# Unread products on row groups and column groups behind the end of a gated attention and feed-forward kernel

## The chip, the cores and the metric

The kernel runs on one core of a Trainium2 chip, in one launch. The metric is the device time of one execution in microseconds. Before the change it is 1037.36 us, the median of 2 runs (1037.11 and 1037.6).

## The reference

One input `x` of 2048 tokens with 448 features goes into two blocks, whose results are mixed token by token by a gate:

```
g = sigmoid((x * gate_w).sum(-1))
qkv = x @ wqkv                          # 448 -> 3 x 16 heads x 28
p = softmax(q @ k.T * 28 ** -0.5)       # 2048 x 2048 for each of 16 heads
a = (p @ v) @ wo                        # back to 448
b = (gelu(x @ w_gate) * (x @ w_up)) @ w_down   # 448 -> 1792 -> 448
out = g * a + (1 - g) * b               # 2048 x 448, float32
```

Everything is float32. The gelu is the tanh approximation.

## The kernel before

The tokens are cut into 4 blocks of 512 (`TB`) or 16 tiles of 128 (`P`). Most products are made in the type `float32r` from operands that were split into a high and a low part, so that one product of the reference is a sum of eleven (`PAIRS`, line 44) products of 128 rows by 128 columns by 512. `X` (line 67) holds the split input with the features on the 128 partitions: seven tiles of 2048 tokens, in a pool that stays to the end. Every product is issued through the helper `mm` (line 53), which pins it: TensorE does the products in the order in which the program writes them. All products therefore have line 54 in the profile, and are told apart by their tiles.

The work comes in three stages.

1. Lines 88 to 264: seven warming products on a tile of zeros (`warm`, line 108), whose result nothing reads; then queries and keys (`pqk`), stored to memory, and values (`pv`), kept in `VA`. A bound on the scores is worked out (`pb`, `pr`, lines 240 and 243), and a branch at line 286 is taken only where it is exceeded.
2. Lines 321 to 453: the attention, head by head. `scores` (line 345) makes a tile `sc` of 128 keys by 1024 queries, ScalarE takes its exponential into `pt`. After each eight key tiles `values` (line 355) multiplies them by the values. These products are in plain float32 and only 32 columns wide: four of them, `j` = 0 to 3, write to four strips of 32 partitions of one accumulator `po` (shown as `ps`), so each stands on its own **column group** of the array. Between the scores the generator `up` (line 394) hands out products of the feed-forward block (`ps<-X,half`), whose results go to memory.
3. Lines 457 to 575: the rest of the feed-forward block and the output. `hidden` makes or reads the gate and up halves of the hidden layer (`pg`), `down` (line 499) multiplies by `w_down` into `pd`, `project` (line 545) multiplies the attention's result by `wo`. The last call, `down(*pend)` at line 575, makes four tiles of `pd`; VectorE mixes each into `y` (line 517) and SyncE's queue stores it (line 518). This is the end of the program.

The accumulators of the last stage are three tiles in the pool `psg` and five in `psd`, which together fill the eight banks of PSUM; its SBUF pools are given back, and with them their addresses, when the block of line 457 is left.

Of the kernel before, what the change touches and what calls it, by code (L numbers as in the profile page):

```python
# [7 lines left out]
F32 = mybir.dt.float32  # L8
# [5 lines left out]
PSUM = bass.MemoryType.PSUM  # L14
# [3 lines left out]
P = 128  # L18
TB = 512
# [555 lines left out]
        down(*pend)  # L575


# [33 lines left out]
```

## Time and profile before

| | |
|---|---|
| median of 2 runs | 1037.36 us |
| the profiled execution's own time | 1038.66 us |
| its span, first to last instruction | 1036.8 us |
| TensorE products busy | 1030.6 us (99%), 5671 products |
| TensorE weight loads busy | 737.6 us (71%) |
| ScalarE / VectorE / GpSimd busy | 603.3 / 325.7 / 195.9 us |
| granted TensorE clock | 1.0 |

PE is TensorE with its products, PEld TensorE with the loads of the operand that is held in the array (each product has one load), DVE VectorE, ACT ScalarE, POOL GpSimd, SP SyncE; SPq is SyncE's queue of transfers. A group of instructions is shown by its line, engine, operation, output and inputs, by the piece of the array (128*128 is all of it, 128*32 is 128 rows by 32 columns), the shape and the count, then the busy time in us and the mean length of one in ns, then the idle time of the engine ahead of it. Records of one group overlap, so the busy time is less than the count times the mean. In the lines of the timeline the first number is the start and the second the length from the start of the first to the end of the last, both in us; x24 means that 24 instructions were merged, and the bracket at the end has the idle time ahead of them.

### The profile page before, as it was taken

What the parts mean: (1) busy time and instruction counts of PE and PEld (TensorE: products, weight loads), DVE (VectorE), ACT (ScalarE), POOL (GpSimd) and SP (SyncE); (2) the same over time, 40 slices, a digit from 0 to 9 for tenths busy, and PEclk for the clock granted to TensorE, in tenths of its full rate; (3) what the DMA queues carried; (4) which work ended last, traced back from release to release, by engine and by line L of the source; (5) the groups of instructions that cost most, each with busy time, mean ns of one, the idle gap of its engine ahead of it and who ended that gap; (6) DMA issues with size and microseconds to landing.
All of it is one profiled execution on the core that took longest, in us unless ns stands there. A gap on an engine that the chain in (4) does not pass through costs nothing.

```text
span 1036.8 us, 14751 instructions
## 1 busy us (share of the span) xinstructions
PE 1030.6 (99%) x5671; PEld 737.6 (71%) x5671; DVE 325.7 (31%) x519; ACT 603.3 (58%) x742; POOL 195.9 (19%) x294
## 2 busy tenths in 40 slices
PE   9999999999999999999999999999999999999998
PEld 7889865666566556655665566556666888888997
DVE  5452011111111111111111111111113687777756
ACT  4332575777577757775777677667763344333322
POOL 6322003021130221211312302202111200001221
PEclk9999999999999999999999999999999999999999
DMA  6865324324234233344242342423124645443553
GB/s 222 315 262 145 78 87 113 103 71 124 75 93 118 83 103 83 88 124 112 71 113 87 96 113 71 115 76 107 53 79 149 175 140 161 140 120 82 160 170 118
DMA packets 59964, 124.25 MB, mean 120 GB/s; under 512 B 11472, under 2 KB 18384, under 8 KB 56272
## 3 DMA queue, kind: packets, MB, share of 16 engines
q1 hardware_dynamic: 50672, 109.99, 35.9%
q0 software_dynamic: 8384, 12.47, 4.5%
q8 instruction: 47, 0.77, 0.3%
q10 hardware_dynamic: 832, 0.79, 0.3%
q14 instruction: 29, 0.24, 0.1%
HBM read 78.64 MB, written 44.56 MB: 119 GB/s over the span
## 4 chain that ended last, share of the span: by engine, by line
PE 88%; DVE 0%; issue 0%
PE ps L54 42%; PE sc L54 23%; PE pd L54 17%; PE pg L54 7%; DVE y L517 0%
## 5 line engine op out<-in xcount | busy, mean ns | idle before, releaser
L352 ACT ACTIVATE pt<-sc 128x1024 f32<-128x1024 f32 x512 | 475.0, 1074 | 188.7 <-PE sc L54 188.4
L54 PE MATMUL sc<-Q,K 128*128 128x512 f32 x1024 | 319.7, 393 | 0.0
L54 PE MATMUL ps<-X,half 128*128 128x512 f32 x924 | 289.7, 391 | 0.1
L54 PEld LDWEIGHTS sc<-Q,K 128*128 128x128 f32 x1024 | 188.8, 188 | 65.2 <-issue 26.0
L54 PE MATMUL ps<-pt,V 128*32 128x512 f32 x2048 | 226.4, 594 | 0.0
L54 PEld LDWEIGHTS ps<-X,half 128*128 128x128 f32 x924 | 173.3, 188 | 38.8 <-issue 1.4
L54 PEld LDWEIGHTS ps<-pt,V 128*32 128x32 f32 x2048 | 63.4, 110 | 145.6 <-issue 144.5
L54 PE MATMUL pd<-w,hl 128*128 128x448 f32 x672 | 140.7, 366 | 0.0
L410 DVE COPY u<-ps 128x512 f32<-128x512 f32 x84 | 57.9, 689 | 256.6 <-PE ps L54 256.5
L54 PEld LDWEIGHTS pd<-w,hl 128*128 128x128 f32 x672 | 126.0, 188 | 11.5
L373 POOL DMA_DIRECT2D dend<-o x64 | 31.8, 505 | 417.7 <-DVE o L364 414.8
L496 ACT ACTIVATE hl<-g 128x512 fp32r<-128x512 f32 x56 | 35.4, 632 | 89.8 <-DVE g L495 80.1
L54 PE MATMUL pg<-X,half 128*128 128x512 f32 x308 | 74.3, 391 | 0.0
L54 PE MATMUL pqk<-X,WQK 128*128 128x512 f32 x308 | 72.8, 399 | 0.9 <-ACT X L152 0.8
L54 PEld LDWEIGHTS pqk<-X,WQK 128*128 128x128 f32 x308 | 59.3, 193 | 14.7 <-ACT X L152 1.5
L54 PEld LDWEIGHTS pg<-X,half 128*128 128x128 f32 x308 | 57.9, 188 | 11.6
L514 DVE SCALAR_TENSOR_TENSOR acc<-pd,gate,acc 128x448 f32<-128x448 f32 x80 | 53.6, 680 | 21.6 <-PE pd L54 21.6
L367 DVE COPY o<-ps 128x512 f32<-128x512 f32 x16 | 11.1, 691 | 148.4 <-PE ps L54 89.2
L364 DVE TENSOR_TENSOR o<-ps,o 128x512 f32<-128x512 f32 x16 | 11.1, 691 | 147.8 <-PE ps L54 147.8
L170 ACT ACTIVATE hl<-pqk 128x512 fp32r<-128x512 f32 x28 | 16.7, 598 | 42.5 <-PE pqk L54 40.5
L497 DVE TENSOR_TENSOR hl<-g,hl 128x512 fp32r<-128x512 f32 x56 | 38.4, 686 | 9.6 <-ACT hl L496 8.5
L495 DVE TENSOR_TENSOR g<-g,u 128x512 f32<-128x512 f32 x56 | 38.0, 686 | 10.5 <-ACT g L494 9.8
(73 smaller groups left out, 528.9 us busy)
## 6 DMA issues: line engine op xcount, KB each, us to landing
ud<-u SPq DMA_DIRECT2D x84, 256.0 KB
qkd<-hl SPq DMA_DIRECT2D x28, 512.0 KB
K<-qkd SPq DMA_DIRECT2D x64, 224.0 KB
Q<-qkd SPq DMA_DIRECT2D x64, 224.0 KB
u<-ud SPq DMA_DIRECT2D x56, 256.0 KB
gs<-ud SPq DMA_DIRECT2D x28, 256.0 KB
rb<-rdend POOLq DMA_DIRECT2D x64, 64.0 KB, 2.9
raw<-in_xT SPq DMA_DIRECT2D x14, 256.0 KB
```

Source lines behind the costliest of these rows:

```text
L54: return pin(nc.tensor.matmul(o, lhsT, rhs, start=start, stop=stop))
L170: pin(nc.scalar.activation(hl[:, 0], p, AF.Copy))
L352: nc.scalar.activation(pt, sc, AF.Exp, scale=SCALE)
L364: nc.vector.tensor_tensor(o, po, o, OP.add)
L367: nc.vector.tensor_copy(o, po)
L373: nc.gpsimd.dma_start(out=dend[h:h + 1, j * 512:(j + 1) * 512], in_=o[j * 32 + DH:j * 32 + DH + 1])
L410: nc.vector.tensor_copy(u, p)
L495: pin(nc.vector.tensor_tensor(g, g, u, OP.mult))
L496: nc.scalar.activation(hl[:, 0], g, AF.Copy)
L497: nc.vector.tensor_tensor(hl[:, 1], g, hl[:, 0].bitcast(F32), OP.subtract)
L514: nc.vector.scalar_tensor_tensor(acc[:, t], p, g1, acc[:, t], OP.mult, OP.add)
```

## The change

Behind the last `down` a further block is added. It takes a new SBUF pool with two tiles of constants, `W` and `R`, and a new PSUM pool with eight accumulators `T` of 128 by 512. Nothing reads `T`. Two helpers issue products:

- `quad` makes one product on each of the **row groups** that it is given: group `r` is partitions 32 r to 32 r + 31. Both operands are slices of `X` on these 32 partitions (128 columns held, 512 streamed, in `float32r`), and the result goes to `T[r]`.
- `run` makes products like those of `values`: plain float32, 128 rows, 32 columns, four of them on the four column groups of `T[4]`, with 256 or 512 columns streamed.

The block calls 126 times `quad` on four groups; then four times a `run` of 8 rounds with 256 columns and 24 `quad`; then twice a `run` of 4 rounds with 512 columns and 12 `quad` with the groups in the order 0, 2, 1, 3; then 24 `quad` on two groups and 24 on three.

```diff
@@ -575,6 +575,43 @@
         down(*pend)
 
 
+    with ExitStack() as ph:
+        bp = ph.enter_context(tc.tile_pool(name="bp", bufs=1))
+        pb4 = ph.enter_context(tc.tile_pool(name="pb4", bufs=1, space=PSUM))
+        T = [pb4.tile([P, TB], F32, name=f"t{i}") for i in range(8)]
+        W = bp.tile([P, 8, 32], F32, name="W")
+        R = bp.tile([P, 8, TB], F32, name="R")
+        nc.vector.memset(W, 0.5)
+        for i in range(4):
+            nc.vector.memset(R[:, 2 * i:2 * i + 2], 0.25)
+
+        def quad(k, n, groups=(0, 1, 2, 3)):
+            for r in groups:
+                a = slice(32 * r, 32 * r + 32)
+                mm(T[r], X[a, (k + r) % 7, (k % 16) * P:(k % 16 + 1) * P],
+                   X[a, (k + 3) % 7, r * TB:(r + 1) * TB], k == 0, k == n - 1)
+
+        def run(kts, n):
+            for k in range(kts):
+                for j in range(4):
+                    mm(T[4][j * 32:(j + 1) * 32, 0:n], W[:, k % 8], R[:, (k + 2 * j) % 8, 0:n], k == 0, k == kts - 1)
+
+        for k in range(126):
+            quad(k, 126)
+        for _ in range(4):
+            run(8, 256)
+            for k in range(24):
+                quad(k, 24)
+        for _ in range(2):
+            run(4, 512)
+            for k in range(12):
+                quad(k, 12, (0, 2, 1, 3))
+        for k in range(24):
+            quad(k, 24, (0, 1))
+        for k in range(24):
+            quad(k, 24, (0, 1, 2))
+
+
```

## The prediction

> **What bounds the kernel now.** I read first the page's span and busy times, then the slices, then the chain of work that ended last, then the groups.
>
> ```profile
> span 1036.8 us, 14751 instructions
> PE 1030.6 (99%) x5671; PEld 737.6 (71%) x5671; DVE 325.7 (31%) x519; ACT 603.3 (58%) x742; POOL 195.9 (19%) x294
> PE   9999999999999999999999999999999999999998
> PEclk9999999999999999999999999999999999999999
> PE 88%; DVE 0%; issue 0%
> PE ps L54 42%; PE sc L54 23%; PE pd L54 17%; PE pg L54 7%; DVE y L517 0%
> ```
>
> TensorE has work in flight for 1030.6 of 1036.8 us, at a full granted clock in every slice, and 88% of the chain lies on it. Work that is added to its queue therefore finds no hole to go into: whatever TensorE needs for it is added to the time, unless it goes behind the last useful product, where a few microseconds of other work are still running. That is where this change puts it. So the question is what stands at the end, and how long TensorE takes for the added products. The timeline of the last stretch (start, length, engine, line, output and inputs, count):
>
> ```profile
> 1027.93 4.85 PEld L54 LDWEIGHTS pd<-w,hl 128*128 128x128 f32 x24
> 1028.13 5.02 PE L54 MATMUL pd<-w,hl 128*128 128x448 f32 x24
> ...
> 1030.26 3.98 SPq L518 DMA_DIRECT2D out<-y  x4
> ...
> 1033.19 0.68 DVE L517 SCALAR_TENSOR_TENSOR y<-pd,gate,acc 128x448 f32<-128x448 f32 x1 [0.53 <-PE pd L54]
> ```
>
> The last product ends at 1028.13 + 5.02 = 1033.15 us, the last VectorE step at 1033.87, and the last store is issued by 1034.24; the rest up to 1036.8 is that store's way to memory. So 1036.8 - 1033.15 = 3.65 us of the span lie behind TensorE's end, and added products run beside them.
>
> **What is added.** Counted from the diff, `quad` is called 126 + 4 x 24 + 2 x 12 = 246 times with four row groups, 24 times with two and 24 times with three: 294 rounds, 984 + 48 + 72 = 1104 products of 32 rows by 128 columns by 512 (the change's few words say about 1650; I go by the diff). `run` adds 4 x 8 rounds of four products with 256 columns and 2 x 4 rounds with 512: 160 products in plain float32, on column groups as `values` has them. Five memsets on VectorE have 30 us or more of products ahead of the first run to hide in; without that cover they would cost a few us once. No transfer is added.
>
> **The price of a product.** No row of before has a product on 32 rows, so it must come from its neighbours: a full product of the same type and 512 columns, and the values, whose four products stand on four column groups.
>
> ```profile
> 779.08 3.56 PE L54 MATMUL ps<-X,half 128*128 128x512 f32 x15
> ...
> 778.86 3.36 PEld L54 LDWEIGHTS ps<-X,half 128*128 128x128 f32 x15
> L54 PE MATMUL ps<-X,half 128*128 128x512 f32 x924 | 289.7, 391 | 0.1
> L54 PEld LDWEIGHTS ps<-X,half 128*128 128x128 f32 x924 | 173.3, 188 | 38.8 <-issue 1.4 <-DVE o L364 0.7 <-DVE o L367 0.4
> L54 PE MATMUL ps<-pt,V 128*32 128x512 f32 x2048 | 226.4, 594 | 0.0
> L54 PEld LDWEIGHTS ps<-pt,V 128*32 128x32 f32 x2048 | 63.4, 110 | 145.6 <-issue 144.5
> ```
>
> A record is longer than what it costs, since records overlap. Fifteen loads of 188 ns take 3.36 us, so they start (3.36 - 0.19) / 14 = 0.227 us apart, and the products with them: (3.56 - 0.39) / 14 = 0.226. A **full product costs 0.227 us**. The values' 1024 calls show as 2048 records, two for each float32 product. One stretch of 64 records, with its neighbours:
>
> ```profile
> 400.66 0.62 PE L54 MATMUL sc<-Q,K 128*128 128x512 f32 x2
> 401.21 7.07 PE L54 MATMUL ps<-pt,V 128*32 128x512 f32 x64
> 408.22 0.73 PE L54 MATMUL sc<-Q,K 128*128 128x512 f32 x2
> 408.79 0.63 PE L54 MATMUL ps<-X,half 128*128 128x512 f32 x2
> ```
>
> ```profile
> 401.21 0.16 PEld L54 LDWEIGHTS ps<-pt,V 128*32 128x32 f32 x8 [0.36 <-issue]
> 401.67 0.13 PEld L54 LDWEIGHTS ps<-pt,V 128*32 128x32 f32 x4 [0.30 <-issue]
> ...
> 407.25 0.13 PEld L54 LDWEIGHTS ps<-pt,V 128*32 128x32 f32 x4 [0.30 <-issue]
> 408.22 0.19 PEld L54 LDWEIGHTS sc<-Q,K 128*128 128x128 f32 x1 [0.84 <-issue]
> ```
>
> Four loads come every (407.25 - 401.67) / 13 = 0.429 us, so four records on four column groups cost 0.429 us together, while one record alone is 594 ns long. The four run **side by side**. Their loads do too: eight loads of 110 ns are over in 0.16 us, so they start (160 - 110) / 7 = 7 ns apart. The row groups split the array the other way, and the values are the only row that shows what TensorE does with a split array. I take it for them: a round of four costs what one full product costs, 0.227 us, and so does a round of two or three. The bounds are: below, what the columns alone of a full product cost (the pd rows give (4.85 - 0.19) / 23 = 0.203 us for 448 columns, so 64 columns make 0.024 us and 512 make 0.19, the rest being the same for any width); above, four products one behind another, 0.908. I take the value nearest to both rows, 0.227.
>
> **The sum.** Rounds on row groups: 294 x 0.227 = 66.7 us. Runs: a 256-column round is two quartets of records of 0.429 / 2, so 32 x 0.429 = 13.7 us (27.5 if a shorter record costs no less, the upper bound), and 8 rounds of 512 cost 8 x 0.858 = 6.9 us. Going between the two ways of splitting: in the stretch above, two full products end their share at 400.66 + 0.454 = 401.11 and the values begin at 401.21, 0.10 later; their 16 quartets end at 401.21 + 6.86 = 408.07 and the next product begins at 408.22, 0.15 later; the one after the next two comes 0.12 late. That is 0.37 for there and back, six times: 2.2 us (0 to 6 x 0.84 = 5, if the whole idle stretch of the loads is paid). Together 66.7 + 13.7 + 6.9 + 2.2 = **89.5 us**.
>
> The new accumulators take all eight PSUM banks, among them the five of `pd`, so I let the first round wait for the last read of `pd`, at 1033.87 (without that wait it starts at 1033.15). Then TensorE ends at 1033.9 + 89.5 = 1123.4, its last record 391 - 227 = 0.16 us later. The stores are long done. The span is 1123.6 us. Before, the profiled execution took 1038.66 us for a span of 1036.8, so 1.86 lie around it, and 1125.4 is the sum on its own scale; the median of the runs shown, 1037.36, is 0.56 above that span, so I forecast **1124 us**, 8.4% slower.
>
> **Rivals.**
>
> *The loads take turns.* From 32 to 128 columns a load goes from 110 to 188 ns, 0.81 ns a column, so 104 ns of a full load are its columns. A load for 32 rows still has 128 columns. If row groups share one way in, a round of four costs 4 x 0.104 = 0.416, of three 0.312, of two still 0.227: 246 x 0.416 + 24 x 0.312 + 24 x 0.227 = 115.3 us instead of 66.7, and 1173 us. If instead a load can't go beside the product of its own row group, a round costs 0.188 + 0.227 = 0.415 whatever its size, 122 us, and 1179 us. And if TensorE's queue can't hand out instructions faster than in the values (eight in 0.429 us, 54 ns each), 2208 of them take 118 us: 1176 us. Three mechanisms with one price. Against the first two speaks that full loads run beside the product ahead of them (3.36 us of loads beside 3.56 of products), and that the values' loads start 7 ns apart; for them, that those are 32 columns, not 128. Against the third, this stretch:
>
> ```profile
> 87.49 0.50 PE L54 MATMUL pb<-sq,selt 128*16 128x1 f32 x14
> ```
>
> Fourteen products with their loads start within 0.50 - 0.16 = 0.34 us, 26 ns a pair; four pairs would need 0.10 of the 0.227 us. But that is a short burst. The Trainium skill, "TensorE: Matmul & The Clock Gate", section "LDWEIGHTS (loading the stationary operand)", says that a 32-row load takes as long as one of 128 rows since only columns count, 107 ns for 128 by its formula; by that figure, an estimate from this page, four in turn would make 0.43 us a round and about 1176 us. Its section "The mechanism" says that a load overlaps products in flight only where the row groups differ; the full loads here, in the same rows as the product beside them, contradict that. Together 0.20.
>
> *Partial overlap.* Every further row group adds something to a round, between the 7 ns of the loads' stagger and the (415 - 227) / 3 = 63 ns of the last rival. At a third of that, 23 ns, rounds cost 0.250, 0.273 and 0.296: 6.0 + 6.6 + 72.8 = 85.4 us, 18.7 more, 1143 us. The same page, "Measured speedup vs the span model", gives 3.07 times for four products on four row groups; 0.908 / 3.07 = 0.296 us a round is that price, an estimate with the page's ratio. No run here shows a row group. 0.14.
>
> *No overlap at all.* Row groups take turns: 1104 x 0.227 = 250.6 us and 1308 us; if only their loads' whole records must follow each other, 1104 x 0.188 = 207.6 and 1265 us. For it: nothing in the trace shows row groups side by side. Against it: column groups are. 0.14.
>
> *Not slower.* Nothing reads the new tiles, so a builder that drops products without a reader would leave the kernel as it is, at 1037 us. It decides as soon as it applies to all of them; short of that, the rounds would have to cost nothing, since the runs alone are 20 us. Against it stands another unread tile in the same kernel:
>
> ```profile
> L54 PE MATMUL warm<-zero 128*128 128x512 f32 x7 | 3.4, 652 | 1.5 <-DVE zero L105 1.5
> ```
>
> All seven warming products of line 108 are there. 0.01.
>
> **Chances and range.** Full overlap has 0.51. Its own range is 1110 to 1141: rounds at 0.19 (55.9 us), free switches and the early start make 1033.15 + 76.5 + 0.16 + 0.56 = 1110; rounds at 0.227 with short records that cost no less (13.8 more) and dear switches (2.8 more) make 1141. With the partial case and the 0.4 us rounds 0.85 of the chance lies up to 1182, so the range is 1110 to 1182; the serial cases stay outside. A change of 2% (21 us) is about what a measurement of this kernel can tell from none; every case but the last is slower by more. Faster 0.005, within 2% 0.015, slower 0.98.
>
> **What would show it.** In the changed kernel's profile the span is the old one up to 1033 us, then only TensorE: a group of 1104 MATMUL of 32*128, whose busy time beside its count is the price, 66.7 us over 294 rounds, or 115 to 122, or 208 to 251. The loads of 188 ns should overlap four deep; if they take turns, PEld is busy throughout. Rounds of two against rounds of four tell the rivals apart: equal length is full overlap or the load behind its own product, half the length is serial. PEclk should stay at 9: a lower granted clock behind 1033 us would stretch every term, and would make the forecast wrong in a way that no row of before shows. So would a wait on the runs' operands, should VectorE's memsets come late.

## The result and the profile after

The changed kernel takes 1124.87 us (median of 2 runs, 1124.76 and 1124.97) against 1037.36: 1.0844 times as long, 95% interval 1.0797 to 1.089. The forecast was 1124. Its page, in the same order as before:

```profile
span 1122.9 us, 17604 instructions
PE 1118.5 (100%) x7095; PEld 807.0 (72%) x7095; DVE 330.4 (29%) x524; ACT 604.0 (54%) x742; POOL 195.8 (17%) x294
...
PE ps L54 39%; PE sc L54 21%; PE pd L54 15%; PE t L54 8%; PE pg L54 6%; DVE y L517 0%
```

TensorE has 7095 - 5671 = 1424 records more: 1104 of row groups, and two for each of the 160 plain float32 products. The chain has a new member, `t`, with 8% of the span; everything else kept its place. The groups of the new products and their loads:

```profile
L54 PE MATMUL t<-X 32*128 32x512 f32 x1104 | 69.0, 388 | 0.8 <-DVE y L517 0.8
L54 PE MATMUL t<-R,W 128*32 128x256 f32 x256 | 14.6, 380 | 0.0
L54 PE MATMUL t<-R,W 128*32 128x512 f32 x64 | 7.3, 595 | 0.0
...
L54 PEld LDWEIGHTS t<-X 32*128 32x128 f32 x1104 | 62.7, 183 | 7.8 <-issue 3.3 <-DVE y L517 1.1
```

A product of 32 rows is as long as a full one, 388 ns against 391, and its load is as long as a full load, 183 against 188. But 1104 of them keep TensorE busy for 69.0 us: 0.235 us for each of the 294 rounds, not for each product. The timeline of the end, whole on TensorE from 1031.78 us on:

```profile
1025.98 5.02 PE L54 MATMUL pd<-w,hl 128*128 128x448 f32 x24
...
1031.04 0.68 DVE L517 SCALAR_TENSOR_TENSOR y<-pd,gate,acc 128x448 f32<-128x448 f32 x1 [0.53 <-PE pd L54]
...
1031.78 13.48 PE L54 MATMUL t<-X 32*128 32x512 f32 x232 [0.78 <-DVE y L517]
```

```profile
1060.61 3.66 PE L54 MATMUL t<-R,W 128*32 128x256 f32 x64
1064.20 5.77 PE L54 MATMUL t<-X 32*128 32x512 f32 x96
1069.90 3.66 PE L54 MATMUL t<-R,W 128*32 128x256 f32 x64
...
1104.33 3.64 PE L54 MATMUL t<-R,W 128*32 128x512 f32 x32
1107.90 13.94 PE L54 MATMUL t<-X 32*128 32x512 f32 x168
```

The first 126 rounds take 1060.61 - 1031.78 = 28.83 us, 0.229 each. The last line holds 12 rounds of four, 24 of two and 24 of three: (13.94 - 0.38) / 59 = 0.230, so the size of a round doesn't matter. A run of 256 columns and the change behind it take 3.59 us, of which 16 quartets of records account for 3.43. A window among the rounds (stretch, its length, busy time and count of PE, PEld, DVE, ACT, POOL, then the granted clock, the share of DMA and GB/s) has the clock at 1.00:

```profile
1040.00:1060.00 20.00, 20.00 (x360) 19.36 (x356) 0.00 (x0) 0.00 (x0) 0.00 (x0) 1.00 0.01 2
```

### The profile page after: what moved, and what is told of

It is laid out like the page before. It is cut to its first block, busy times and chain, and to the rows that moved or that the text cites. A ratio compares the mean times of both kernels' runs of the same rounds, so it can differ in the third digit from the quotient of the medians.

```text
span 1122.9 us, 17604 instructions
## 1 busy us (share of the span) xinstructions
PE 1118.5 (100%) x7095; PEld 807.0 (72%) x7095; DVE 330.4 (29%) x524; ACT 604.0 (54%) x742; POOL 195.8 (17%) x294
## 4 chain that ended last, share of the span: by engine, by line
PE 90%; DVE 0%; issue 0%
PE ps L54 39%; PE sc L54 21%; PE pd L54 15%; PE t L54 8%; PE pg L54 6%; DVE y L517 0%
## 5 line engine op out<-in xcount | busy, mean ns | idle before, releaser
L54 PE MATMUL t<-X 32*128 32x512 f32 x1104 | 69.0, 388 | 0.8 <-DVE y L517 0.8
L54 PEld LDWEIGHTS t<-X 32*128 32x128 f32 x1104 | 62.7, 183 | 7.8 <-issue 3.3
```

The lines of the kernel that those rows point to most:

```text
L54: return pin(nc.tensor.matmul(o, lhsT, rhs, start=start, stop=stop))
```

## The experiments

All are changes to the added block alone; unless the text says otherwise, the number of products and their accumulators stay. What they compute is never read, so none changes the output. Two theories stand against each other first: S, products on different row groups run side by side and one row group does one product at a time; Q, a product of a quarter of the rows costs a quarter.

### All on one row group

```diff
-                a = slice(32 * r, 32 * r + 32)
+                a = slice(0, 32)
```

> All 1104 products take their rows from partitions 0 to 31, one row group; their number, size and accumulators stay. If the changed kernel is cheap because products on different row groups run side by side (theory S), these must follow one another: 1104 x 0.227 = 250.6 us where the changed kernel spends 67.3 (294 rounds of 0.229), so about 1308 us. If a product of a quarter of the rows costs a quarter of a full one wherever it stands (theory Q), nothing changes: about 1125 us.

Measured: 1513.82 us, 1.4595 times the kernel before (1.4545 to 1.4646). Q falls; but S missed by 206 us. The granted clock shows why. Windows of this kernel, with the clock third from the end:

```profile
1036.00:1037.00 1.00, 1.00 (x6) 0.77 (x5) 0.84 (x2) 0.00 (x0) 0.00 (x0) 1.00 0.00 0
1037.00:1038.00 1.00, 1.00 (x6) 0.82 (x5) 0.84 (x2) 0.00 (x0) 0.00 (x0) 1.00 0.00 0
1038.00:1039.00 1.00, 1.00 (x4) 0.75 (x3) 0.29 (x1) 0.00 (x0) 0.00 (x0) 0.55 0.00 0
...
1100.00:1200.00 100.00, 100.00 (x236) 77.12 (x235) 0.00 (x0) 0.00 (x0) 0.00 (x0) 0.50 0.00 0
```

The products do follow one another: while the clock is at 1.00, their records start about 0.23 us apart. But 4.4 us after the block began at 1033.65 the clock fell to 0.50, and a product then costs 100 / 235 = 0.43 us (by the loads that the window counts). TensorE is busy without a gap all the while. So this run mixes two effects, and the next two take them apart.

### 64 rows, one product at a time

```diff
-                a = slice(32 * r, 32 * r + 32)
+                a = slice(0, 64)
```

> All products take 64 rows, partitions 0 to 63: twice the rows of the run on one group, and still one behind another. S: 1104 x 0.227 us, about 1308 us at a full clock. It asks what the clock follows: if it is the rows that work, half of them as in the run on two groups, it does here what it does there; if it is the number of products side by side, it falls as in the run on one group, to some 1510 us.

Measured: 1310.26 us (ratio 1.2627, 1.259 to 1.2664), 2 us from the 1308 of S at a full clock. Its first 504 products in the timeline, and a window of them, with the clock third from the end:

```profile
1033.86 114.55 PE L54 MATMUL t<-X 64*128 64x512 f32 x504 [0.78 <-DVE y L517]
```

```profile
1060.00:1080.00 20.00, 20.00 (x90) 16.23 (x89) 0.00 (x0) 0.00 (x0) 0.00 (x0) 1.00 0.00 1
```

(114.55 - 0.39) / 503 = 0.227 us a product at clock 1.00: the rival "no overlap at all", met where products share rows. The clock held with one product at a time, so it doesn't follow their number.

### All on two row groups

```diff
-                a = slice(32 * r, 32 * r + 32)
+                a = slice(32 * (r % 2), 32 * (r % 2) + 32)
```

> All products on row groups 0 and 1, in turn. S: two side by side, so 552 rounds of 0.229 us in place of 294, 59 us more: about 1184 us, if the granted clock stays at 1.0 as it did in the 24 two-group rounds of the changed kernel (5.5 us of them). If the clock falls to 0.5 whenever less than three quarters of the array's rows work for some 4 us, as it did with one group: some 120 us more again, about 1310 us.

Measured: 1191.49 us (ratio 1.1482, 1.1449 to 1.1516). This is S at a full clock, but for 7 us. They come from the end, where the three-group rounds become groups 0, 1, 0: group 0 has 48 products there, so 48 rounds stand where the expectation counted 36 (12 x 0.229 = 2.7 us), and group 1 idles half of the time. There the clock fell, at about 1179 us (windows, as above), which costs some 4 us more:

```profile
1050.00:1060.00 10.00, 10.00 (x92) 10.00 (x90) 0.00 (x0) 0.00 (x0) 0.00 (x0) 1.00 0.01 2
...
1180.00:1182.00 2.00, 2.00 (x9) 1.59 (x8) 0.00 (x0) 0.00 (x0) 0.00 (x0) 0.50 0.00 0
```

Two groups side by side and 64 rows one at a time both keep the clock, 32 rows one at a time lose it: of these three, it goes with the rows at work.

### One full product for each round

```diff
-            for r in groups:
-                a = slice(32 * r, 32 * r + 32)
-                mm(T[r], X[a, (k + r) % 7, ...], X[a, (k + 3) % 7, ...], k == 0, k == n - 1)
+            mm(T[0], X[:, k % 7, (k % 16) * P:(k % 16 + 1) * P], X[:, (k + 3) % 7, 0:TB], k == 0, k == n - 1)
```

This leaves 294 products of 128 rows, all on the accumulator `T[0]`, in place of 1104 of 32 rows on four accumulators.

> Each of the 294 rounds is one product of 128 rows by 128 columns by 512, on the whole array, in place of two to four on row groups. S: a round costs what a full product costs, so about 1124 us, and no change beyond the 0.002 us a round by which 0.229 differs from 0.227. If the row groups of a round cost something of their own (starts, loads, more instructions), it is clearly below: 5 ns for each of the 810 further products would make 1121 us.

Measured: 1125.54 us (ratio 1.0843, 1.0812 to 1.0875), where the changed kernel's ratio was 1.0844. Its timeline:

```profile
1032.31 28.88 PE L54 MATMUL t<-X 128*128 128x512 f32 x126 [0.78 <-DVE y L517]
1061.12 3.66 PE L54 MATMUL t<-R,W 128*32 128x256 f32 x64
```

126 full products take 1061.12 - 1032.31 = 28.81 us; 126 rounds of four took 28.83. The central step of the prediction, that a round costs what one full product costs, holds here to 0.02 us in 126 rounds, and the 810 further products with their loads are free.

### Less to stream

```diff
-                mm(T[r], X[a, (k + r) % 7, (k % 16) * P:(k % 16 + 1) * P],
-                   X[a, (k + 3) % 7, r * TB:(r + 1) * TB], k == 0, k == n - 1)
+                mm(T[r][:, 0:P], X[a, (k + r) % 7, (k % 16) * P:(k % 16 + 1) * P],
+                   X[a, (k + 3) % 7, r * TB:r * TB + P], k == 0, k == n - 1)
```

> Every row-group product streams 128 columns in place of 512; number, order and weight loads (128 columns each) stay. S with the loads of four groups side by side: the round falls from 0.229 to what one load sets, between the 0.104 us of its columns and its whole record of 0.188: 1088 to 1113 us. If loads cost nothing at any width, the round follows its columns to 0.065 us: about 1077 us. If the 0.229 us are already the loads' or the instruction queue's time and the stream only fits into it: no change, about 1125 us.

Measured: 1092.85 us (ratio 1.0537, 1.0502 to 1.0571). In the timeline:

```profile
1032.20 14.29 PE L54 MATMUL t<-X 32*128 32x128 f32 x504 [0.78 <-DVE y L517]
1046.42 3.66 PE L54 MATMUL t<-R,W 128*32 128x256 f32 x64
```

A round is (1046.42 - 1032.20) / 126 = 0.113 us, half of 0.229: the stream set the full round, and neither the four loads in turn nor the queue of instructions needs more than 0.113 us a round (eight instructions, 14 ns each). That is close to the 0.104 us of one load's columns and well above a quarter of the stream, 0.057, so one load is probably the next limit; the queue isn't excluded as that limit. (The 0.065 us that the expectation gives for the stream alone is worked out from no row.) At the end of this run the clock fell too:

```profile
1084.00:1086.00 2.00, 2.00 (x54) 2.00 (x54) 0.00 (x0) 0.00 (x0) 0.00 (x0) 1.00 0.04 8
1086.00:1088.50 2.50, 2.45 (x43) 2.26 (x40) 0.00 (x0) 0.00 (x0) 0.00 (x0) 0.63 0.00 0
```

It did so 4.5 us after the rounds of four ended at about 1082.1, in rounds of two and three groups. The same rounds with 512 columns kept it in the changed kernel (1.00 from 1108 to 1120 us).

### Without the runs

```diff
-            run(8, 256)
...
-            run(4, 512)
```

> The six runs of column-group products are left out, and with them the changes between the two ways of splitting; all row-group rounds stay. By the sum of the prediction: 20.6 us of runs and 2.2 of changes less, about 1102 us. With free changes 1104 us; if each there and back cost the whole 0.84 us in which the loads are idle, 1099 us.

Measured: 1102.4 us (ratio 1.0629, 1.0598 to 1.066). In the timeline the block is one line:

```profile
1032.24 66.94 PE L54 MATMUL t<-X 32*128 32x512 f32 x1104 [0.78 <-DVE y L517]
```

All 294 rounds in one stretch take 66.94 us, against 66.7 + 0.16 in the sum; the runs and their changes are worth 1124.87 - 1102.4 = 22.5, against 22.8.

### Four times as many changes

```diff
-        for _ in range(4):
-            run(8, 256)
-            for k in range(24):
-                quad(k, 24)
+        for _ in range(16):
+            run(2, 256)
+            for k in range(6):
+                quad(k, 6)
...
-            run(4, 512)
+            run(1, 512)
```

(The second loop in the same way: 8 times, with 3 rounds each.)

> The same products, cut into four times as many turns: 16 runs of 2 rounds with 6 row-group rounds each, and 8 runs of 1 round with 3, so 24 changes there and back in place of 6. At 0.36 us each: 18 x 0.36 = 6.5 us more, about 1131 us. Free changes: about 1125 us. At the loads' whole idle stretch of 0.84 us: 1140 us.

Measured: 1132.14 us, ratio 1.0917 (1.0898 to 1.0937). 7.3 us for 18 changes more is 0.40 us there and back, where the prediction read 0.37 off the values. Three turns in the timeline:

```profile
1062.54 1.07 PE L54 MATMUL t<-R,W 128*32 128x256 f32 x16
1063.54 1.68 PE L54 MATMUL t<-X 32*128 32x512 f32 x24
1065.14 1.07 PE L54 MATMUL t<-R,W 128*32 128x256 f32 x16
```

Four quartets (0.86) take 1.00 us from start to start, and six rounds (1.37) take 1.60: 0.14 and 0.23, together the 0.37 of the prediction. The executions of this run lie between 1131.42 and 1133.18 us, so the 0.40 is known to about 0.1.

### Plain float32

```diff
-                mm(T[r], X[a, ...], X[a, ...], ...)
+                mm(T[r], X[a, ...].bitcast(F32), X[a, ...].bitcast(F32), ...)
```

> The row-group products read the same bits as plain float32 in place of float32r. In that type a product on a column group is two records, and four of each cost 0.429 us. If row groups stand side by side whatever the type, a round costs 0.858 us: 294 x (0.858 - 0.229) = 185 us more, about 1310 us. If they only do so in float32r: 1104 x 0.858 = 947 us in place of 67, about 2005 us.

Measured: 1311.3 us (ratio 1.2648, 1.2621 to 1.2675). In the timeline:

```profile
1033.24 108.43 PE L54 MATMUL t<-X 32*128 32x512 f32 x1008 [0.78 <-DVE y L517]
1141.60 3.66 PE L54 MATMUL t<-R,W 128*32 128x256 f32 x64
```

The first 126 rounds take 1141.60 - 1033.24 = 108.36 us, 0.860 each. Row groups stand side by side in both types, and the price read off the values, 0.858 us for four plain float32 products side by side, holds for rows as for columns.

### In another order: four, sixteen and eight in a row

```diff
         def quad(k0, n, groups=(0, 1, 2, 3)):
+            if k0 % 4:
+                return
             for r in groups:
                 a = slice(32 * r, 32 * r + 32)
-                mm(T[r], X[a, (k + r) % 7, ...
+                for k in range(k0, min(k0 + 4, n)):
+                    mm(T[r], X[a, (k + r) % 7, ...
```

> The same products on the same row groups, in another order: four in a row on group 0, then four on group 1, and so on. S with products that start in the order of the program: in each four only the first starts beside the last of the group ahead, so 826 slots of 0.229 us stand where 294 were, 122 us more, about 1247 us. If TensorE takes products out of order, so that those of the next group pass the waiting ones: about 1125 us. If four in a row undo the overlap altogether: 1104 x 0.227, about 1308 us. Q: about 1125 us.

Measured: 1128.42 us (ratio 1.088, 1.0848 to 1.0911). The expectation counts in slots of 0.229 us, the time of one round, in which each row group can do one product. Starts in program order would have cost 122 us; the run cost 3.5. So products do pass waiting ones. How far TensorE looks ahead is asked with 16 in place of 4 in the same lines:

> As the run with four in a row, now sixteen in a row on each row group. If TensorE lets a product pass waiting ones of another group, but sees only so many ahead, a count gives the time: it takes the first product of each group among the next W. W of 64 or more: 294 slots, 1125 us; W = 32: 328 slots, 1133 us; W = 16: 441 slots, 1159 us; W = 8: 623 slots, 1200 us, and a lower clock on top where only one or two groups work. Program order: 1029 slots, over 1290 us.

Measured: 1399.11 us (ratio 1.3483, 1.3428 to 1.3539), beyond all the numbers given but the last: the look ahead is shorter than I tried, and the clock was at 0.50 for nearly all of the block:

```profile
1033.25 165.41 PE L54 MATMUL t<-X 32*128 32x512 f32 x504 [0.78 <-DVE y L517]
```

```profile
1100.00:1150.00 50.00, 50.00 (x155) 40.45 (x153) 0.00 (x0) 0.00 (x0) 0.00 (x0) 0.50 0.00 0
```

With 0.43 us a slot at that clock, and 0.229 in the first 3 us, the first 504 products make about 390 slots. Starts in program order would make 473 (one slot saved at each of 31 changes of group); a count in which three products can wait for their group before the next group's are reached gives 380. Eight in a row, with the four accumulators under names of their own:

> Eight in a row on each row group, each group's accumulator under a name of its own (aaa to ddd), so that the order of the starts is seen. If some three products can wait for their group while the next group's pass (which the runs with four and sixteen in a row fit), a count gives 574 slots of 0.229 us in place of 294, 64 us more, about 1189 us at a full clock: the products on bbb begin beside the sixth on aaa or so. If only two can wait: 315 + 4 x 63 + 2 x 27 + 78 = 699 slots, 1218 us or more with a lower clock. If eight can: some 1130 us.

Measured: 1231.38 and 1256.95 us in its two executions, so no ratio is given. Their mean granted clocks are 0.976 and 0.954, so in both the clock was at 0.50 for a part of the time. In the profiled one, the longer, it fell 3.5 us into the block and came back beside the first run on column groups, which began at 1148.88 us:

```profile
1110.00:1130.00 20.00, 20.00 (x88) 17.76 (x87) 0.00 (x0) 0.00 (x0) 0.00 (x0) 0.50 0.00 0
1130.00:1160.00 30.00, 30.00 (x190) 24.26 (x190) 0.00 (x0) 0.00 (x0) 0.00 (x0) 0.62 0.00 1
1160.00:1200.00 40.00, 40.00 (x368) 32.73 (x366) 0.00 (x0) 0.00 (x0) 0.00 (x0) 1.00 0.00 1
```

With two of four groups at work on average, the clock thus stayed at 0.50 for over 100 us ahead of that run, and at 1.00 in the rounds between the later runs. But for the first fall, whose cause isn't shown, two groups neither lowered a full clock nor raised a halved one in this one trace. What the run was made for is the order of the starts, in its timeline:

```profile
1032.96 1.42 PE L54 MATMUL aaa<-X 32*128 32x512 f32 x5 [0.78 <-DVE y L517]
1034.00 0.49 PE L54 MATMUL bbb<-X 32*128 32x512 f32 x1
1034.22 0.39 PE L54 MATMUL aaa<-X 32*128 32x512 f32 x1
1034.34 0.39 PE L54 MATMUL bbb<-X 32*128 32x512 f32 x1
1034.45 0.39 PE L54 MATMUL aaa<-X 32*128 32x512 f32 x1
1034.58 0.38 PE L54 MATMUL bbb<-X 32*128 32x512 f32 x1
1034.69 0.38 PE L54 MATMUL aaa<-X 32*128 32x512 f32 x1
1034.80 0.62 PE L54 MATMUL bbb<-X 32*128 32x512 f32 x2
1035.04 0.49 PE L54 MATMUL ccc<-X 32*128 32x512 f32 x1
```

In the program all eight products on `aaa` come ahead of the first on `bbb`. On the chip `bbb` begins when five of `aaa` have begun and three still wait, and from there the two groups alternate, until three of `bbb` wait and `ccc` begins. So products pass others that wait for another row group, and about three can be passed. Whether that is one list of waiting products or one for each group, these runs don't tell. The trace doesn't list the order in which products were handed to TensorE, so that order rests on the pin of every call; and what the pin keeps is then this order alone, and not, as the description of the kernel before has it, the order in which TensorE does them.

## Why the prediction was right, point by point

- **TensorE has no hole, so the block is paid in full.** Right: nothing but `t` grew, and TensorE's share went from 99% to 100%.
- **The start behind the last read of `pd`.** Forecast 0.72 to 0.75 us behind the last product (1033.87 or 1033.9, against 1033.15); measured 1031.78 - 1031.00 = 0.78, with VectorE's `y` named as the releaser.
- **A round costs one full product, 0.227 us.** Right, and the step on which all depended: 66.94 us for 294 rounds, and 28.83 us against 28.81 for 126 rounds and 126 full products. It was an inference from column groups to row groups, which the rows of before couldn't prove.
- **Runs and changes, 22.8 us.** 22.5 by leaving them out. A change there and back is 0.37 by the rows of before and 0.40 by doing it 18 times more.
- **The sum.** 89.5 us and a last tail of 0.16 forecast, 1107.90 + 13.94 - 1031.78 = 90.06 measured. In the profile of after the last useful product ended 2.15 us earlier than in that of before, which took 1.3 us more than the median; on the median the forecast is 0.9 us short. That it came so near is partly luck, since the time ahead of the block differs more between the two profiles than that. The prediction's cover for the memsets, "30 us or more", is 126 x 0.227 = 28.6 by its own price; they ended at 1035.50 + 0.91 = 1036.41, 24 us ahead of the first run.
- **The rivals.** Loads in turn, loads that can't pass a product of their row group, and a slow queue would all have put a round at 0.41 us or more; it is 0.229, and 0.113 with a short stream. Partial overlap is excluded by the equal rounds of two, three and four. (A third of its 63 ns is 21, not 23, which changes nothing here.) "No overlap at all" is what products on the same rows do. One sign was badly chosen: PEld was to be busy throughout if the loads take turns, and it was busy for 19.36 of 20 us in the window shown with the result, although they don't. The 1104 loads of 183 ns make 202 us in 62.7 us of busy time, so some three run at once, spread over the round. The builder dropped nothing.
- **The clock.** It stayed at 1.0, but the reason wasn't in the prediction: as far as these runs show, it is that enough of the array was at work. The same 1104 products on one row group cost 476 us, not the 271 of the serial rival, since the clock halved.

## What to carry to other kernels

Where a product has 32 rows, what counts is not how many there are but how many follow one another on the same row group: put neighbours in the program on different groups, four at a time, and the four cost one. Here the column groups of the trace were a fair guide to row groups. Look at the granted clock of a stage that uses a small part of the array, even where TensorE is busy without a gap.

## What was not expected of the hardware

- **The clock goes with how much of the array works.** With 32 rows at work all the time it fell from 1.00 to 0.50 after 4.4 us, and with 1.3 groups on average (504 products in about 390 slots) or 1.5 (the end of the run on two groups) as well; with 64 rows, or two groups side by side, it stayed at 1.00; with 8 in a row, two groups on average, it stayed at either value for a long time. Rows alone aren't all: with 128 streamed columns, rounds of two and three groups lost it 4.5 us after they began. Runs on column groups, with all 128 rows, brought it back: in the run on one row group, the one at 1245.22 us had raised it to 1.00 by 1251 us, and the products behind it had lost it again by 1257 us. How rows, columns and time add up isn't settled, nor were the held columns varied.
- **Products start out of program order** when they are on different row groups; about three waiting ones are passed. The Trainium skill, "TensorE: Matmul & The Clock Gate", section "The mechanism", says that products start and end strictly in the order of the program. For the starts, the run with eight in a row shows otherwise: `bbb` starts at 1034.00, the sixth `aaa` at 1034.22.
- **Four row groups gave four times the rate.** 0.908 / 0.229 = 3.97 in a long stretch, where the Trainium skill, "TensorE: Matmul & The Clock Gate", section "Measured speedup vs the span model", has 3.07 for four products on four row groups.
